# Step priorities, a decay table from one matmul, two FFN2 tiles in borrowed banks and wider warm-up matmuls in a fused attention and FFN kernel

## The chip, the cores and the metric

One core of one Trainium2 chip. Times are device microseconds of one execution of the whole kernel. Every experiment was timed beside fresh runs of the kernel before on the same chip. A ratio is the mean time of one kernel's fast runs over the mean time of the other's fast runs of the same rounds, so it is not quite the ratio of the medians quoted beside it; a bracket behind a ratio is its 95% interval. A single run counts as slow when it is more than 1.5% above the fastest run of the same kernel.

## The reference

Linear attention with a decay per head, in blocks of 64 positions, and behind it an FFN of 3072 tokens with a snake activation:

```python
# q, k, v: (4 batches, 8 heads, 768 positions, 64); lam: 8 decays near 0.98
for b in range(nb):                       # 12 blocks of 64
    intra = (qb @ kb.T * Dmask) @ vb      # Dmask[i, j] = lam ** (i - j), i >= j
    inter = (qb * lam_pow) @ kv_state
    out[block b] = intra + inter
    kv_state = lam_block * kv_state + (kb * rev_pow).T @ vb
# x: attention output as 3072 x 512; w_in 512 x 2048; w_out 2048 x 512
h = x @ w_in
g = h + sin(alpha * h) ** 2 / (alpha + 1e-9)
return g @ w_out
```

## The kernel before

The kernel cuts attention into 24 units (a batch, half of the heads, two blocks of 128 positions) and the FFN into 6 groups of 512 tokens. Four units make the input of one group. For a unit, ACT or POOL casts q and k, POOL scales v by powers of the decay (`vb`), PE turns q and k (`pt`), forms the state (`kp`, or `okv` where it uses that bank) and the scores (`sp`), DVE masks, and PE adds the inter and the intra part into `okv`. A group is 16 FFN1 tiles (`hps`), a sine, a square and a sum for each, and 4 FFN2 tiles (`ops`) of 16 matmuls each.

The Python code does not emit instructions in written order. Each step is put into a list with an estimated cost, its predecessors, the banks that it takes and a priority; a planner simulates the engines and emits each engine's steps in the order found. This matters in what follows: in the traces of this case a step that was late held up what stood behind it on its engine (ACT did no other work in the 1.36 us for which it waited for one tile, and PE none in the 1.40 us for which it waited for another, both below).

```python
class Plan:
    def run(self):
        # (cut) for each engine: of the ready steps whose banks are free,
        # take the one with the lowest priority value op.vt, and emit it
```

The decay table is made at the start from lam, which a DMA brings in. `E` holds powers of lam by position (partition) and head. The kernel needs them along the free axis on all partitions, `et`, and PE does that with 16 small fp32 matmuls, which the trace counts as x32 (two records for each of them; the prediction calls them 32 matmuls):

```python
    def tables(op):
        G.tensor_tensor(out=E[:, 0], in0=lam_bc[:], in1=pos[:].to_broadcast([P, H]), op=ALU.pow)
    def tables_v(op):
        V.tensor_tensor(out=E[:, 1], in0=E[:, 0], in1=lam_bc[:], op=ALU.mult)
        V.reciprocal(out=R[:], in_=E[:])
    def tables_t(op, hp):                 # four times, hp = 0..3
        # (cut)
        for par in range(2):
            for hd in range(2):
                h = 2 * hp + hd
                nc.tensor.matmul(out=tb0.tile[half[hd], hp, par, :],
                                 lhsT=E[:D, par, h:h + 1].to_broadcast([D, D]),
                                 rhs=idf[:], start=True, stop=True)
    def tables_l(op):                     # LBD: the decay of a whole block, needed for every state
        for hd in range(2):
            V.tensor_copy(out=LBD[half[hd], :, hd], in_=tb0.tile[half[hd], :, 1, D - 1])
```

The other parts that the change touches:

```python
    KVF = {0, 1, 2}                       # units whose state matmul uses FFN banks, not okv
    NWARM = 22; NFILL = 30; FLAG = .12    # matmuls on zeros: at the start, and in later idle time
    bd = kvp.tile([P, 2, 2, D], BF16, name=f"kvbd{b}{hh}{c}")          # decayed state
    def f2mm(op, first, g, m, j, cols=slice(0, DM)):                   # FFN2
        if j == 0:
            op.tile = bank(op, "f", [P, DM], FP32, "ops")              # one of four FFN banks
        # (cut)
```

## Time and profile before

| | kernel before |
|---|---|
| time | 220.83 us median of 3 runs (220.65 to 220.99) |
| span in the profile | 218.9 us |
| first FFN1 matmul | 22.5 us |
| start of the part in which PE has no gap | 76.4 us |
| last matmul ends | 214.8 us |

The prediction below shows how the page, the chain, the stretches and the waits of PE were read. One part of the start-up got less attention in it than it deserved, so here it is. In the timeline of a kernel each line has the start, the length, the engine, the source line, the operation, output and input names, shapes and the number of instructions; a bracket tells how long the engine sat idle just before, and whose end released it. First PE, then DVE:

```profile
6.67 1.15 PE L323 MATMUL et<-idf,E 64*64 64x64 f32 x32
7.75 0.40 PE L399 MATMUL pt<-iden,qk 128*128 128x128 bf16 x4
8.26 0.32 PE L456 MATMUL kp<-vb,qk 64*64 64x64 bf16 x16
```

```profile
7.86 0.33 DVE L329 COPY LBD<-et 64x4 f32<-64x4 f32 x2 [0.93 <-PE et L323]
```

The table is on its way at 6.67 us and `LBD` is there from 7.86. The first unit's state matmul (`kp`) follows at 8.26. PE does not idle in these lines.

### The profile page before, as it was taken

What the parts mean: (1) busy time and instruction counts of PE and PEld (TensorE: products, weight loads), DVE (VectorE), ACT (ScalarE), POOL (GpSimd) and SP (SyncE); (2) the same over time, 40 slices, a digit from 0 to 9 for tenths busy, and PEclk for the clock granted to TensorE, in tenths of its full rate; (3) what the DMA queues carried; (4) which work ended last, traced back from release to release, by engine and by line L of the source; (5) the groups of instructions that cost most, each with busy time, mean ns of one, the idle gap of its engine ahead of it and who ended that gap; (6) DMA issues with size and microseconds to landing.
All of it is one profiled execution on the core that took longest, in us unless ns stands there. A gap on an engine that the chain in (4) does not pass through costs nothing.

```text
span 218.9 us, 5315 instructions
## 1 busy us (share of the span) xinstructions
PE 207.5 (95%) x2083; PEld 108.4 (50%) x2109; DVE 121.2 (55%) x191; ACT 144.4 (66%) x255; POOL 123.1 (56%) x202
## 2 busy tenths in 40 slices
PE   8888998999999899999999999999999999999992
PEld 5656543455454354545545545554554444444461
DVE  1575986446475793777547647547646544354000
ACT  3867798873688747777567677686767676786120
POOL 5659999849869999999997545303111101101000
PEclk9999999999999999999999999999999999999998
DMA  4999999999999996893999953532022022210423
GB/s 126 293 283 251 206 199 207 261 278 268 211 202 259 218 267 129 240 279 77 197 273 230 267 144 76 47 72 48 5 48 49 1 49 48 48 32 19 96 64 81
DMA packets 62809, 33.65 MB, mean 154 GB/s; under 512 B 18608, under 2 KB 59840, under 8 KB 62784
## 3 DMA queue, kind: packets, MB, share of 16 engines
q1 hardware_dynamic: 57776, 29.04, 59.0%
q0 software_dynamic: 4752, 4.19, 12.0%
q8 instruction: 16, 0.26, 0.5%
q10 hardware_dynamic: 256, 0.08, 0.2%
q14 instruction: 9, 0.07, 0.1%
HBM read 27.28 MB, written 6.29 MB: 153 GB/s over the span
## 4 chain that ended last, share of the span: by engine, by line
PE 80%; POOL 6%; DMA 6%; issue 2%; ACT 2%; DVE 2%; SPq 1%; ACTq 0%; POOLq 0%
PE ops L603 38%; PE hps L575 33%; DMA st_v<-in_v_dram 3%; PE sp L422 3%; DMA st_q<-in_q_dram 3%; PE okv L545 2%; PE okv L532 2%; POOL vb L386 2%; POOL s L591 1%; PE okv L456 1%; PE pt L399 1%; DVE gall L594 1%; POOL kvbd L484 1%; SPq L364 1%; PE bz L654 1%
## 5 line engine op out<-in xcount | busy, mean ns | idle before, releaser
L594 DVE SCALAR_TENSOR_TENSOR gall<-s,r_sb,hps 128x512 bf16<-128x512 bf16 x96 | 70.6, 746 | 62.5 <-ACT s L589 43.8
L575 PE MATMUL hps<-xt,w_in_sb 128*128 128x512 bf16 x364 | 93.5, 379 | 2.2 <-DVE gall L594 1.0
L603 PE MATMUL ops<-w_out_sb,gall 128*128 128x512 bf16 (+1 forms) x394 | 93.6, 370 | 0.5 <-PE okv L456 0.2
L582 ACT ACTIVATE s<-hps,alpha_sb 128x512 bf16<-128x512 f32 x96 | 65.2, 684 | 34.6 <-PE hps L575 32.9
L603 PEld LDWEIGHTS <-gall 128*128 128x128 bf16 x400 | 38.6, 98 | 42.5 <-issue 0.3
L575 PEld LDWEIGHTS <-w_in_sb 128*128 128x128 bf16 x384 | 35.9, 98 | 43.3 <-issue 2.3
L591 POOL TENSOR_TENSOR s<-s 128x512 bf16<-128x512 bf16 x23 | 23.8, 1039 | 43.9 <-ACT s L582 43.8
L589 ACT ACTIVATE s<-s 128x512 bf16<-128x512 bf16 x73 | 45.7, 630 | 2.0
L431 DVE TENSOR_TENSOR sm<-sp,mask 128x512 bf16<-128x512 f32 x48 | 32.4, 684 | 3.9 <-PE sp L422 3.6
L386 POOL TENSOR_TENSOR vb<-st_v,R 128x512 bf16<-128x512 f32 x24 | 25.0, 1045 | 3.9 <-DMA st_v<-in_v_dram 3.7
L484 POOL TENSOR_TENSOR kvbd<-kvx,LBD 128x256 bf16<-128x256 f32 x32 | 19.6, 612 | 4.3 <-PE okv L532 1.8
L481 POOL TENSOR_TENSOR kvx<-kva,kvs 128x128 f32<-128x128 f32 x32 | 14.5, 454 | 13.1 <-ACT kva L466 12.9
L609 ACT COPY ob<-ops 128x512 f32<-128x512 f32 x23 | 13.2, 573 | 10.2 <-PE ops L603 6.6
L562 DVE TENSOR_TENSOR xt<-okv,ET 128x512 bf16<-128x512 f32 x24 | 16.4, 685 | 4.1 <-PE okv L545 3.6
L380 POOL CAST qk<-st_k 128x512 bf16<-128x512 f32 x20 | 12.2, 610 | 3.5 <-DMA st_k<-in_k_dram 3.5
L380 POOL CAST qk<-st_q 128x512 bf16<-128x512 f32 x16 | 9.8, 610 | 4.8 <-PE okv L456 4.4
L654 PE MATMUL bz<-zeros 128*128 128x256 bf16 x52 | 11.1, 336 | 1.1 <-DVE warm L274 1.1
L466 ACT COPY kva<-okv 128x256 f32<-128x256 f32 (+1 forms) x16 | 5.1, 318 | 9.7 <-PE okv L456 9.7
L405 ACT COPY qt<-pt 128x512 bf16<-128x512 bf16 x14 | 8.1, 587 | 4.2 <-PE pt L399 4.0
L532 PE MATMUL okv<-qt,kvbd 128*128 128x128 bf16 x80 | 8.8, 219 | 1.5 <-POOL kvbd L484 1.0
L545 PE MATMUL okv<-sm,vb 64*64 64x128 bf16 x384 | 9.9, 218 | 0.2 <-issue 0.2
L422 PE MATMUL sp<-qt 64*64 64x128 bf16 x384 | 10.0, 222 | 0.0
(50 smaller groups left out, 96.7 us busy)
## 6 DMA issues: line engine op xcount, KB each, us to landing
st_q<-in_q_dram SPq DMA_DIRECT2D x24, 256.0 KB, 5.3
st_k<-in_k_dram SPq DMA_DIRECT2D x24, 256.0 KB, 5.5
st_v<-in_v_dram SPq DMA_DIRECT2D x24, 256.0 KB, 5.2
out_dram<-ob SPq DMA_DIRECT2D x46, 128.0 KB, 2.4
w_out_sb<-in_moe_w_out_dram POOLq DMA_DIRECT2D x4, 512.0 KB, 15.6
w_in_sb<-in_moe_w_in_dram POOLq DMA_DIRECT2D x3, 512.0 KB, 10.0
w_in_sb<-in_moe_w_in_dram POOLq DMA_DIRECT2D x1, 384.0 KB, 6.5
qt<-qk SPq DMA_TRANSPOSE x15, 4.4
```

Source lines behind the costliest of these rows:

```text
L380: ENGINE[op.eng].tensor_copy(out=o, in_=i)
L386: ENGINE[op.eng].tensor_tensor(out=T[u, "vb"][:], in0=T[u, "v"][:].rearrange("p h two e -> p two h e"), in1=R[:, :, hs].unsqueeze(3).to_br ...
L422: nc.tensor.matmul(out=T[u, "sp"][hd][half[c], par, hp, :], lhsT=QT[half[hd], 1, par, hp, half[c]], rhs=QT[half[hd], 0, :, hp, half[c]], s ...
L431: V.tensor_tensor(out=T[u, "sm"][:, hd], in0=T[u, "sp"][hd][:], in1=mask[:].unsqueeze(2).to_broadcast([P, 2, 2, P]), op=ALU.mult)
L484: G.tensor_tensor(out=bd[:], in0=X.unsqueeze(2).to_broadcast([P, 2, 2, D]), in1=LBD[:, hs, :].unsqueeze(3).to_broadcast([P, 2, 2, D]), op= ...
L562: V.tensor_tensor(out=xt[g][:, 2 * hh:2 * hh + 2, bb, :, :].rearrange("p hp c i -> p c hp i"), in0=T[u, "op"][:, :, 0:2 * P].rearrange("p ...
L575: op.ins = nc.tensor.matmul(out=op.tile[:, cols], lhsT=w_in_sb[:, c, f * P:(f + 1) * P], rhs=xt[g][:, c].rearrange("p b c i -> p (b c i)") ...
L582: A.activation(out=op.tile[:, cols], in_=mm.tile[:, cols], func=ACTF.Sin, scale=alpha_sb[:, f:f + 1])
L589: A.activation(out=op.tile[:, cols], in_=s1, func=ACTF.Square)
L591: ENGINE[op.eng].tensor_tensor(out=op.tile[:, cols], in0=s1, in1=s1, op=ALU.mult)
L594: V.scalar_tensor_tensor(out=gall[g][:, f, cols], in0=sq.tile[:, cols], scalar=r_sb[:, f:f + 1], in1=mm.tile[:, cols], op0=ALU.mult, op1=A ...
L603: op.ins = nc.tensor.matmul(out=first.tile[:, cols], lhsT=gall[g][:, f, m * P:(m + 1) * P], rhs=w_out_sb[:, f, cols], start=(f == 0), stop ...
```

## The change

The intent is a shorter way from the start to the point where PE is filled with FFN work alone: better step order by a searched table of priority offsets (`TUNE`, some 700 entries; the second value of an entry, where there is one, ties the step to one engine), a table with fewer PE instructions, fewer users of the one attention output bank pair `okv`, and two FFN2 tiles of group 0 in that pair, so that FFN1 keeps its four banks. Cut to its core:

```diff
+    TUNE = {
+        "tab1": (-33.2, None), "tab2": (9.5, None), "tabd": (8.9, None), ...   # cut: some 700
+    }
+    TT = -38; TD = -500                      # priorities of the new table steps
-    NWARM = 22; NFILL = 30; FLAG = .12
+    NWARM = 11; NFILL = 20; FLAG = .25       # the 11 have 512 columns instead of 256
-    KVF = {0, 1, 2}
+    KVF = {0, 1, 2, 3, 4, 5}
-    GATES = {8: ('f', 2), 6: ('o', 0)}       # loads of unit 6 wait for w_out's first quarter
+    GATES = {8: ('f', 8), 5: ('o', 4)}       # loads of unit 5 wait for its second quarter
+    LEND = {0: ('okv', 0), 1: ('okv', 1)}
 ...
-    def tables_t(op, hp):                    # the 16 matmuls shown above
+    def tables_d(op):
+        for hd in range(2):
+            V.tensor_copy(out=E2[half[hd]], in_=E[half[hd]]
+                          .rearrange("p par (hp two) -> p two hp par", two=2)[:, hd])
+        V.tensor_tensor(out=ED[:], in0=idf[:].unsqueeze(1).to_broadcast([P, HP * 2, D]),
+                        in1=E2[:].rearrange("p hp par -> p (hp par)").unsqueeze(2)
+                        .to_broadcast([P, HP * 2, D]), op=ALU.mult)
+    def tables_t(op):
+        op.tile = bank(op, "f", [P, HP, 2, D], FP32, "et")
+        nc.tensor.matmul(out=op.tile[:].rearrange("p hp par i -> p (hp par i)"), lhsT=ones[:],
+                         rhs=ED[:].rearrange("p k i -> p (k i)"), start=True, stop=True)
 ...
-        bd = kvp.tile([P, 2, 2, D], BF16, name=f"kvbd{b}{hh}{c}")
+        bd = kvp.tile([P, 2, 2, D], BF16, name=f"kvbd{b}{hh}{c}{tp if c else 0}")
 ...
     def f2mm(op, first, g, m, j, cols=slice(0, DM)):
-        if j == 0:
+        if j == 0 and op.lent is None:
             op.tile = bank(op, "f", [P, DM], FP32, "ops")
+        elif j == 0:                         # cut: takes half of an okv pair
 ...
+    tbd = add("tabd", on("DVE", .85), [tb2], TD, tables_d)
+    tb0 = add("tab0", on("PE", .88), [tbd], TT, tables_t, take=("f",), lag=PEL, mode="n", ...)
 ...
-                for e, a in (("ACT", 2 * q), ("DVE", 3 * q)):        # last eviction in two copies
+                ev = add("end1", on("DVE", .35), [prev], vt + 4, ...) # in one
 ...
+    for op in plan.ops:
+        if op.name in TUNE:
+            by, on_ = TUNE[op.name]
+            op.vt += by
+            op.cost = [x for x in op.cost if on_ in (None, x[0])]
     for op in plan.run():
         op.emit(op)
```

Left out are the split of an early unit's output into "inter" and "out", the decay of units 0 to 2 on POOL instead of DVE, k casts on ACT, and other numbers of the planner.

## The prediction

> **What bounds the kernel now.** I read the page first: PE is busy for 95% of the span, and the chain of work that ended last is 80% PE. A busy PE is not a PE at its peak, so the second view was the timeline of PE, where the spacing of groups shows the real pace.
>
> ```profile
> span 218.9 us, 5315 instructions
> PE 207.5 (95%) x2083; PEld 108.4 (50%) x2109; DVE 121.2 (55%) x191; ACT 144.4 (66%) x255; POOL 123.1 (56%) x202
> PE 80%; POOL 6%; DMA 6%; issue 2%; ACT 2%; DVE 2%; SPq 1%; ACTq 0%; POOLq 0%
> ...
> 177.55 0.86 PE ops L603 x4
> 178.41 0.86 PE hps L575 x4
> ```
>
> The last two lines are from the chain in order of time: groups of four FFN matmuls start every 0.865 us, 216 ns each. The kernel has 6 groups x 16 tiles x 4 of FFN1 and as many of FFN2, 768 in all: 768 x 0.216 = 165.9 us. No part of the change touches that. From 76.4 us to the last matmul at 214.8 us the PE timeline has no gap: only FFN groups and attention steps of 1.01 us. So all that can be won lies before 76.4 us or behind 214.8 us.
>
> Third view, busy time by stretches (the second answer is the warm-up tile `bz` alone):
>
> ```profile
> 6.20:22.50 16.30, 14.22 (x336) 10.09 (x335) 11.31 (x24) 11.92 (x27) 11.86 (x15) 1.00 1.19 272
> 22.50:36.40 13.90, 12.79 (x131) 6.07 (x123) 10.87 (x18) 11.93 (x23) 12.93 (x20) 1.00 1.24 205
> 55.80:76.40 20.60, 19.05 (x225) 9.51 (x228) 13.77 (x22) 16.54 (x29) 17.89 (x30) 1.00 1.19 218
> ...
> 6.20:22.50 16.30, 5.73 (x27) 1.00 1.19 272
> ```
>
> The columns are PE, PEld, DVE, ACT, POOL, clock, DMA share and GB/s. From 6.2 us (first transposes) to 22.5 us (first FFN1) PE looks 87% busy, but 5.73 us of that is warm-up on zeros. In 22.5 to 36.4 us ACT (86%) and POOL (93%) are close to full too: they could become the next bound.
>
> Fourth, the timeline of PE shows the waits that PE really has:
>
> ```profile
> 17.61 0.32 PE L456 MATMUL okv<-vb,qk 64*64 64x64 bf16 x16 [0.50 <-POOL vb L386]
> 18.92 0.27 PE L532 MATMUL okv<-qt,kvbd 128*128 128x128 bf16 x2 [0.22 <-ACT kva L510]
> 20.69 0.27 PE L532 MATMUL okv<-qt,kvbd 128*128 128x128 bf16 x2
> ...
> 36.38 1.02 PE L575 MATMUL hps<-xt,w_in_sb 128*128 128x512 bf16 x4 [0.81 <-DVE gall L594]
> 67.68 0.34 PE L532 MATMUL okv<-qt,kvbd 128*128 128x128 bf16 x3 [0.47 <-POOL kvbd L484]
> 73.35 0.34 PE L532 MATMUL okv<-qt,kvbd 128*128 128x128 bf16 x3 [0.56 <-POOL kvbd L484]
> ```
>
> The first three lines are the way to the first FFN1: unit 3's state matmul takes the one `okv` buffer at 17.61, so the output of unit 2, whose second mask was done at 16.8, starts only at 18.92; its eviction ends at 20.3, and unit 3's output follows at 20.69. One buffer passes three users in turn.
>
> [...]the first 24 warm-ups of 256 columns took 5.08 us, 212 ns each, later ones near 110 ns[...] Here unit 3's v took 6.64 us to land, against a median of 5.2 us of its kind, with the first weight load issued 1.0 us after it.
>
> **The change, part by part.**
> 1. *State matmuls of units 3 to 5 in FFN banks (units 0 to 2 have them there already), early output split into "inter" and "out".* Unit 3 no longer holds `okv`. I work the way anew: v3 lands at 16.4 as before; the scaling by R 1.05 gives 17.56; state matmul 0.35 to 17.95; decay on DVE 0.43 to 18.45; inter and out 0.6 behind the masks (unit 3's transposed k is there at 17.3, scores 0.4, two masks 1.3: 19.05) to 19.5; eviction 0.69 to 20.2. The first full FFN1 tile starts at 20.3 instead of 22.5: 2.2 us. The first weight load moves behind unit 2's scaling, so v3 may land up to 1 us earlier; I count none of it. But work done before 22.5 now (unit 4's transposes, scores and state) partly slides behind. By waste: before, 16.3 us less 6.4 (four units at about 1.6), 1.3 (units 4 and 5) and 1.15 (table) is 7.4 us wasted; after, 20.3 - 6.2 = 14.1 less 6.4, 0.9 table, 0.8 of unit 4 and 0.4 for the half FFN1 tile is 5.6. **Gain 1.8**, from 1 to 3.
> 2. *Loads reordered.* Unit 5 waits for the second quarter of w_out, where before unit 6 waited for the first. One unit less is 0.79 MB, 2.7 us at the 290 GB/s of the first stretches, by which the weights come earlier. FFN1 of tile 1 now waits for its weights till about 24; this lets the 1.8 us stand. No own gain.
> 3. *Two FFN2 tiles of group 0 in the two `okv` banks.* FFN1 keeps all four FFN banks while these two tiles accumulate; FFN2 matmuls fill the waits for `gall`. It can remove the 0.81 us at 36.38. **Gain 0.7.** Price: no attention step can use `okv` until both are evicted.
> 4. *Decay tiles of chunk 1 with their own buffer per step.* POOL idled 1.82 us before a decay at 62.99 because PE still read the old one; the next two PE waits, 0.47 and 0.56, are for such tiles. **Gain 0.9.**
> 5. *Priorities, some 700 offsets.* They move no work on or off the kernel, only order. PE idles 2.6 us between 22.5 and 76.4, 1.6 of it counted above. By difference PE spends 2.5 us more there on changes between kinds of work: 138.4 us after 76.4 less 12.8 of steps is 581 FFN matmuls, so 187 x 0.216 = 40.4 us lie in the 53.9, with 8.2 of attention and 0.2 of warm-up. An order fitted to this may take 1.5 of the 3.5 left. **Gain 1.0** after a deduction for an order that fits the planner better than the chip.
> 6. *Table by one matmul.* It removes 32 matmuls (1.15 us) and adds a DVE product of about 0.7 us and one fp32 matmul of 512 columns, 0.9 us by the change's own step cost; no row of the trace has it. The table stands some 0.8 us later, at 9.7 us, and unit 0's eviction needs it at 12.0. **No change.**
> 7. *Tail.* The last two evictions run one after the other (0.27 on ACT, 0.29 on DVE, from 214.79 to 215.38). One DVE copy of 256 columns, about 0.35: **gain 0.2.** The flight of the last output, 3.5 us, stays.
>
> Sum 1.8 + 0.7 + 0.9 + 1.0 + 0.2 = 4.6. I add 0.3 for an earlier v3: 220.8 - 4.9 = **215.9 us**.
>
> **Rivals.** *A. ACT takes PE's place.* All k casts of units 1 to 7 go to ACT, 0.62 us each, where before POOL did some, and the first three states are copied there. ACT already has 86% in the stretch where FFN1 starts; an FFN1 tile wants 0.69 for the sine and 0.63 for the square, 1.32 against PE's 0.865 unless POOL squares. Against it: FFN2 can fill PE once w_out is there, and in 43 to 55 us ACT idles for want of FFN1. If it holds, parts 1 and 5 are lost: about 218.5. *B. The lent banks block attention.* Units 5 to 7 come late now, and `okv` is away: group 1 could start later than today's 55.8. For it: there is one `okv` only. Against it: PE has enough to do, 27.6 us of group 0's FFN, until unit 7 is there, and unit 5 to 7's loads need only 7 to 9 us. It would give 217.5. *C. The loads stay the bound.* DMA runs at 270 to 296 GB/s from 5 to 20 us, and no order of PE makes v3 land earlier. Then only the turn through `okv` is gained: 217. *D. The search hit well*: nearly all idle time and a third of the start-up waste go, 213.5.
>
> **Range and chances.** The parts sum to 215.9, the rivals lie at 217 to 218.5 and at 213.5; eight in ten: 213.6 to 218.6. The 2% line is 220.83 x 0.98 = 216.4, only 0.5 above my centre, so 0.57 faster, 0.41 same. Slower by 2% would need 4.4 us of new waits in a kernel that has under 3 of PE idle time after 22.5: 0.02.
>
> **What would show it.** Right: the first full FFN1 tile at 19.5 to 21 us in the PE timeline; unit 2's output before 18; no PE wait for `gall` above 0.5 near 36; no PE wait for `kvbd` at 60 to 76; the point from which PE has no gap well before 76. Wrong: an ACT or `gall` wait in 20 to 40 us, a PE gap where `okv` is lent, v3 landing later than 16.4, or warm-up matmuls running again behind the first FFN1; and, for the other side, an end below 213.

## The result, and the profile after

The changed kernel took **219.44 us** (median of four runs, 218.51 to 219.60) against 220.74 us of the kernel before (220.59 to 220.99). The ratio is 0.9931 [0.9902, 0.9961]: 0.7% faster, where 2.2% had been predicted; that is short of the 2% line and outside the range on record. A repetition with more runs said nearly the same (below).

The page and the stretches of the changed kernel (columns as in the prediction; the last line is `bz` alone):

```profile
span 217.5 us, 5238 instructions
...
PE 82%; DMA 8%; POOL 4%; ACT 2%; DVE 2%; issue 0%; DVEq 0%; ACTq 0%; POOLq 0%
```

```profile
6.20:22.50 16.30, 13.47 (x302) 8.57 (x303) 12.89 (x28) 10.53 (x27) 12.88 (x17) 1.00 1.13 242
22.50:36.40 13.90, 12.51 (x74) 5.50 (x72) 9.45 (x15) 11.87 (x21) 12.96 (x24) 1.00 1.21 205
55.80:76.40 20.60, 20.05 (x280) 10.48 (x279) 15.96 (x24) 15.71 (x29) 19.73 (x31) 1.00 1.10 241
...
6.20:22.50 16.30, 4.56 (x19) 1.00 1.13 242
```

The last stretch is what was hoped for: PE 97% busy, before 92%. But in 22.5 to 36.4 us, where FFN1 should stand closer, PE is *less* busy (12.51 us, before 12.79; a second profile of the changed kernel has 13.25 there). The PE timeline of the changed kernel shows why:

```profile
9.58 1.10 PE L601 MATMUL et<-ED,ones 128*128 128x512 f32 x2 [1.40 <-DVE ED L595]
10.61 0.32 PE L736 MATMUL kp<-vb,qk 64*64 64x64 bf16 x16
...
21.62 1.93 PE L855 MATMUL hps<-xt,w_in_sb 128*128 128x256 bf16 x12
24.67 4.49 PE L855 MATMUL hps<-xt,w_in_sb 128*128 128x512 bf16 x20 [0.66 <-DMA w_in_sb<-in_moe_w_in_dram]
29.60 3.61 PE L855 MATMUL hps<-xt,w_in_sb 128*128 128x512 bf16 x16 [0.44 <-DVE gall L874]
33.50 1.04 PE L891 MATMUL okv<-w_out_sb,gall 128*128 128x512 bf16 x4 [0.29 <-DMA w_out_sb<-in_moe_w_out_dram]
46.54 0.40 PE L676 MATMUL pt<-iden,qk 128*128 128x128 bf16 x4 [0.72 <-ACT qk L655]
62.63 1.02 PE L855 MATMUL hps<-xt,w_in_sb 128*128 128x512 bf16 x4 [0.55 <-DVE gall L874]
```

Each line but the second and the third begins with a wait that the kernel before did not have. The first is the earliest of them and the longest: PE stands 1.40 us for `ED`, the DVE product of the new table, and the first unit's state matmul comes at 10.61 instead of 8.26. FFN1 begins at 21.62 us instead of 22.5, with one tile in halves, so the first tile that is not in halves comes at about 22.5, the same as before. (The twelve matmuls of that line are eight of the halves and four of the next tile: 8 x 0.108 us, half of the 216 ns of 512 columns, puts the next tile at 22.5, an estimate.) In the profile of the repetition the waits for `ED` (1.39 us), `gall` (0.44 and 0.55) and the q cast (0.72) are there too, the one for w_in is not, and FFN1 begins at 21.27. DVE, then POOL, in the same place:

```profile
7.87 1.56 DVE L595 TENSOR_TENSOR ED<-idf,E 128x512 f32<-128x512 f32 x1
10.72 0.33 DVE L606 COPY LBD<-et 64x4 f32<-64x4 f32 x2 [0.95 <-PE et L601]
```

```profile
7.84 1.04 POOL L663 TENSOR_TENSOR vb<-st_v,R 128x512 bf16<-128x512 f32 x1 [0.33 <-DVE E L593]
```

The product took 1.56 us, not "about 0.7 us". It starts 0.03 us behind POOL's scaling of v, which runs for 1.04 us. `LBD` is there at 10.72, 2.9 us later than before. Only about half of that is the table itself, as an experiment shows: in this run of the changed kernel lam also landed later (the power on POOL began at 5.16 us, before at 4.45). That differs from run to run: the repetition of the change had 4.82.

To compare stretches I counted PE's useful work. Its records overlap (in the first lines shown above that of `et` ends at 7.82 us and the next starts at 7.75), so I took the weight loads of every kind in a stretch, times the steady spacing of that kind, without those of zeros; what is left of the stretch is time without useful work. The differences between kernels are good to about 0.4 us; the levels depend on the spacings taken, and a recount put some of them over 1 us higher. `old_table` is the experiment that follows.

| stretch, us | before | after | `old_table` |
|---|---|---|---|
| 6.2 to 22.5 | 9.3 | 8.4 | 7.65 |
| 22.5 to 36.4 | 1.2 | 1.8 | 0.6 |
| 36.4 to 55.8 | 0.1 | 0.55 | 1.2 |
| 55.8 to 76.4 | 1.3 | 0.1 | 0.0 |
| sum | 11.9 | 10.85 | 9.45 |

So 0.9 us are won ahead of 22.5 us and 0.6 of them given back by 36.4; 0.45 more are given back by 55.8; only the last stretch has its gain. The sum, 1.05 us, and the tail, 0.17 us (one copy of 0.42 us from the last matmul on where two took 0.59), make 1.2; the medians differ by 1.3. For `old_table` the same sum gives 2.6 of 3.3 us.

### The profile page after: what moved, and what is told of

It is laid out like the page before. It is cut to its first block, busy times and chain, and to the rows that moved or that the text cites. A ratio compares the mean times of both kernels' runs of the same rounds, so it can differ in the third digit from the quotient of the medians.

```text
span 217.5 us, 5238 instructions
## 1 busy us (share of the span) xinstructions
PE 206.0 (95%) x2062; PEld 104.5 (48%) x2062; DVE 123.2 (57%) x199; ACT 142.8 (66%) x256; POOL 122.3 (56%) x202
## 4 chain that ended last, share of the span: by engine, by line
PE 82%; DMA 8%; POOL 4%; ACT 2%; DVE 2%; issue 0%; DVEq 0%; ACTq 0%; POOLq 0%
PE ops L891 35%; PE hps L855 34%; DMA w_out_sb<-in_moe_w_out_dram 6%; PE okv L891 3%; PE sp L702 3%; PE okv L825 2%; DMA lam_bc<-in_lam_dram 2%; PE okv L812 2%; POOL w_in_sb L624 1%; POOL vb L663 1%; PE pt L676 1%; PE okv L736 1%; POOL E L584 1%; DVE ED L595 1%; POOL kvbd L764 1%; PE et L601 1%
## 5 line engine op out<-in xcount | busy, mean ns | idle before, releaser
L874 DVE SCALAR_TENSOR_TENSOR gall<-s,r_sb,hps 128x512 bf16<-128x512 bf16 (+1 forms) x97 | 70.0, 740 | 59.1 <-ACT s L869 46.9
L855 PE MATMUL hps<-xt,w_in_sb 128*128 128x512 bf16 (+1 forms) x388 | 90.4, 377 | 1.7 <-DVE gall L874 1.0
L891 PE MATMUL ops<-w_out_sb,gall 128*128 128x512 bf16 (+1 forms) x368 | 82.8, 370 | 0.0
L862 ACT ACTIVATE s<-hps,alpha_sb 128x512 bf16<-128x512 f32 (+1 forms) x97 | 64.5, 677 | 26.9 <-PE hps L855 25.6
L871 POOL TENSOR_TENSOR s<-s 128x512 bf16<-128x512 bf16 (+1 forms) x23 | 23.5, 1022 | 45.1 <-ACT s L862 44.8
L869 ACT ACTIVATE s<-s 128x512 bf16<-128x512 bf16 (+1 forms) x74 | 45.8, 626 | 1.7
L657 POOL CAST qk<-st_k 128x512 bf16<-128x512 f32 x17 | 10.4, 611 | 0.0
L682 ACT COPY qt<-pt 128x512 bf16<-128x512 bf16 x11 | 6.4, 587 | 5.7 <-PE pt L676 5.6
L939 PE MATMUL bz<-zeros 128*128 128x256 bf16 (+1 forms) x31 | 8.8, 371 | 1.3 <-DVE warm L541 1.2
L802 POOL TENSOR_TENSOR kvs<-kvx,ET 128x128 f32<-128x128 f32 x24 | 9.4, 402 | 0.0
```

Of the source, the lines that this page charges most:

```text
L657: ENGINE[op.eng].tensor_copy(out=o, in_=i)
L855: op.ins = nc.tensor.matmul(out=op.tile[:, cols], lhsT=w_in_sb[:, c, f * P:(f + 1) * P], rhs=xt[g][:, c].rearrange("p b c i -> p (b c i)") ...
L862: A.activation(out=op.tile[:, cols], in_=mm.tile[:, cols], func=ACTF.Sin, scale=alpha_sb[:, f:f + 1])
L869: A.activation(out=op.tile[:, cols], in_=s1, func=ACTF.Square)
L871: ENGINE[op.eng].tensor_tensor(out=op.tile[:, cols], in0=s1, in1=s1, op=ALU.mult)
L874: V.scalar_tensor_tensor(out=gall[g][:, f, cols], in0=sq.tile[:, cols], scalar=r_sb[:, f:f + 1], in1=mm.tile[:, cols], op0=ALU.mult, op1=A ...
```

## The experiments

My theory after the two traces was that step 6 of the prediction had failed: the product is slow beside POOL, PE's queue waits for it, and the whole start-up slides. The rivals were that the offsets or the lent banks cost what the rest gains, or that the new waits near 46 us and behind it carry the loss.

**The changed kernel again, five rounds.** No edit.

> The changed kernel once more, unedited, as the yardstick of the runs beside it: 0.993 of the kernel before, 219.2 to 219.6 us, with a span of 217.5 to 217.8 us. If it came out over 1 us away from that, differences under 1 us between kernels would not be readable here.

Measured: 219.28 us median of 11 runs (217.33 to 220.99, one of them slow), ratio 0.9912 [0.9879, 0.9946]. The result stands. New is the spread: 3.7 us, or 3.3 without the slow run, where 45 runs of the kernel before lay within 1.8.

**The old table in the changed kernel.** The planner keeps its costs, so that the order of all steps stays as it was; only what two steps emit differs. The product is still made, once, early and of ones, and nothing reads it: its own time can be seen that way.

```diff
+    V.memset(E2[:], 1.0)
+    V.tensor_tensor(out=ED[:], ...)          # the same product, at the start, unused
     def tables_d(op):
-        # copies into E2, product into ED
+        pass
     def tables_t(op):
         op.tile = bank(op, "f", [P, HP, 2, D], FP32, "et")
-        nc.tensor.matmul(out=..., lhsT=ones[:], rhs=ED[:]..., start=True, stop=True)
+        # the 16 matmuls of before
```

> The changed kernel with every engine's order kept, but the eviction table made by the 32 small matmuls of before; the wide DVE product stays as a measurement, moved on constants to about 3 us, where DVE and GpSimd both have nothing to do. Theory T (the table's lateness, 2.9 us at the decay table, is what ate the gain at the start): LBD is written near 8.8 us instead of 10.7, unit 0's state matmul comes near 8.5 instead of 10.6, the time falls by 0.6 to 1.5 us. Rival P (GpSimd's queue and the landing of the second w_in part near 24.6 us set the first FFN1 tiles): the first microseconds improve, FFN1 still waits to about 24, the time falls by under 0.4 us. The product by itself: 0.6 to 0.7 us if the 1.56 us in the changed kernel came from GpSimd working beside it, 1.5 us if it is the operation itself.

Measured: 217.49 us (four runs from 217.44 to 217.62, one slow one of 221.10), ratio 0.9845 [0.9817, 0.9872]. Its DVE timeline, then its PE timeline:

```profile
2.99 0.69 DVE L592 TENSOR_TENSOR ED<-idf,E 128x512 f32<-128x512 f32 x1 [0.86 <-POOL idf L563]
...
9.38 0.33 DVE L609 COPY LBD<-et 64x4 f32<-64x4 f32 x2 [1.05 <-PE et L603]
```

```profile
20.62 1.91 PE L858 MATMUL hps<-xt,w_in_sb 128*128 128x256 bf16 x11
22.92 4.49 PE L858 MATMUL hps<-xt,w_in_sb 128*128 128x512 bf16 x20
```

The same product takes 0.69 us here, with POOL idle from 2.96 to 5.19 us. `LBD` comes 1.34 us earlier than in the changed kernel (the other 1.5 us of its delay stay: they are the later lam and the new order), the first FFN1 tile 1.00 us earlier, and the DMA wait of 0.66 us is gone from the line at 22.92 (as it is in the repetition of the change). lam was as late here as in the changed kernel (5.19 us), so the gain at the start is the table's. By the medians of the fast runs the kernel is 1.7 us faster than the repetition of the change, in the same rounds.

**The reverse: the new table in the kernel before.**

```diff
-    # 16 matmuls into et
+    # E2 and ED on DVE right behind the reciprocal, one matmul with ones
```

> The kernel before with the table by one matmul and nothing else. The product now starts before GpSimd's scaling of unit 0 and not after it[...]. Theory T: the table stands 1.0 to 1.4 us later and the time rises by 0.4 to 1.2 us. Rival (the start of the kernel before is set by the loads of unit 3, so a late table is absorbed): within 0.2 us of the kernel before.

Measured: 221.93 us (22 runs), ratio 1.0040 [1.0022, 1.0057], that is 0.9 us slower. Part of this is a low clock that came more often (a mean below 0.995 in 8 of the 22 runs, in 5 of 43 of the kernel before); the means of the other runs, 221.43 and 220.89, differ by 0.5. DVE, then POOL:

```profile
6.99 0.69 DVE L327 TENSOR_TENSOR ED<-idf,E 128x512 f32<-128x512 f32 x1
```

```profile
7.27 1.31 POOL L397 TENSOR_TENSOR vb<-st_v,R 128x512 bf16<-128x512 f32 x1 [1.01 <-DMA st_v<-in_v_dram]
```

Here DVE began first, and now the product is quick and POOL's scaling is long: 1.31 us instead of 1.04. Adding up: 6.99 + 0.69 = 7.68, and 7.68 + 1.04 = 8.72, close to the 8.58 at which it ended. In the changed kernel POOL began first: 7.84 + 1.04 = 8.88, and 8.88 + 0.69 = 9.57, close to 9.43. In both, the second ends within 0.14 us of where it would end if it began only when the first was done (an estimate from the lengths of 0.69 and 1.04 us). The new table costs time even in this order. Its `LBD` came at 8.96 us instead of 7.86, but how that reaches the end is not shown: in this one trace FFN1 began at 21.86 us, earlier than the 22.51 of the kernel before.

A later run (`one_decay_buffer`, below) has the order of the changed kernel at the start, and yet its trace shows the other outcome. DVE, then POOL:

```profile
7.46 0.69 DVE L595 TENSOR_TENSOR ED<-idf,E 128x512 f32<-128x512 f32 x1
```

```profile
7.46 1.58 POOL L663 TENSOR_TENSOR vb<-st_v,R 128x512 bf16<-128x512 f32 x1 [0.37 <-DVE E L593]
```

By the record DVE was 0.01 us ahead here, and the product was the quick one; in the other four profiles with this order at the start (two of the change and the two without offsets) POOL was 0.03 to 0.04 us ahead, and the product took 1.55 to 1.56 us. PE then waited 0.39 us for `ED` instead of 1.40. So in these five profiles the product was quick where it started first and slow where POOL started 0.03 to 0.04 us ahead of it. Whether this is a part of its spread was not tested.

**The new table, product first.** If the order decides, then the change can keep its table when DVE makes the product ahead of the reciprocal for which POOL waits.

```diff
     def tables_v(op):
         V.tensor_tensor(out=E[:, 1], in0=E[:, 0], in1=lam_bc[:], op=ALU.mult)
-        V.reciprocal(out=R[:], in_=E[:])
+        # E2 copies and the product into ED, from tables_d
+        V.reciprocal(out=R[:], in_=E[:])
```

> The changed kernel with its table by one matmul and every order kept except on DVE: the product stands ahead of the reciprocal that GpSimd's scaling of unit 0 waits for, so GpSimd cannot be reading then. [...] the table matmul starts near 8.3 us instead of 9.6, the scaling of unit 0 0.6 to 0.9 later, and the time falls by 0.4 to 1.2 us against the changed kernel. If it stays within 0.3 of the changed kernel, the product's collision is not what costs.

Measured: 217.77 us (217.31 to 220.33), ratio 0.9882 [0.9839, 0.9925]. DVE, POOL and PE:

```profile
7.47 0.69 DVE L592 TENSOR_TENSOR ED<-idf,E 128x512 f32<-128x512 f32 x1
```

```profile
8.41 1.04 POOL L664 TENSOR_TENSOR vb<-st_v,R 128x512 bf16<-128x512 f32 x1 [1.37 <-DVE alpha_sb L618]
```

```profile
8.73 1.13 PE L602 MATMUL et<-ED,ones 128*128 128x512 f32 x2
```

Both instructions have their own length now, and `et` starts 0.85 us earlier than in the changed kernel, though POOL's scaling starts 0.57 later. About half of the 0.85 is chance: lam landed 0.43 us earlier in this run (power on POOL at 4.73 us). The median is 1.4 us better than that of the change's fast runs. Two of the six runs are above 219.8 us, with a mean clock of 0.989, so the interval of the ratio still touches that of the change. Among runs with a mean clock of 0.995 or more the means are 217.6 us here (4 of 6), 217.5 with the old table (4 of 5) and 218.7 for the repetition of the change (6 of 11): by these few runs the order of the product gets back what the old table does.

**The offsets off.** The change without `TUNE`.

```diff
-        if op.name in TUNE:
+        if False:
```

> The changed kernel with the per-step priorities taken out (the scheduler falls back on its hand-made ones) and all else kept. If the offsets give what I forecast for them (1.0 us) or more, it runs at 220.4 us or above. If the order that they make costs time on the chip, it runs below 219.

Measured: 220.18 us (22 runs, one slow), ratio 0.9964 [0.9946, 0.9981]. The offsets are worth 0.5% or about 1.1 us (0.9964 against 0.9912, of some 220). The step that gave them 1.0 us had about the right size, though the two intervals meet at 0.9946 and the time is just under the 220.4 us set in advance; they do not cost the gain.

**No own decay buffer for each step.**

```diff
-        bd = kvp.tile(..., name=f"kvbd{b}{hh}{c}{tp if c else 0}")
+        bd = kvp.tile(..., name=f"kvbd{b}{hh}{c}0")
```

> The changed kernel with every engine's order kept, but the decay tiles of chunk 1 with one buffer for all steps, as before. If step 4 of the prediction is right, GpSimd waits again for PE ahead of its decays between 60 and 76 us, PE waits for decay tiles near 67 and 73 us, and the time rises by 0.5 to 1.2 us. Rival (the new order alone removed those waits, the buffer does nothing): within 0.3 us of the changed kernel.

Measured: 218.83 us (19 runs, one slow), ratio 0.9895 [0.9871, 0.9918], not distinct from the change. Its trace has no PE or POOL wait for `kvbd` between 55 and 77 us either. So those waits are gone, as predicted, but not by the buffer. Nor are they back in the trace without offsets. Which part of the change removed them stays open.

**Nothing lent.** With the offsets on, the plan without `LEND` was found to deadlock before it could run, so here nothing is lent and the offsets are off as well; it is to be compared with the run without offsets.

```diff
-    LEND = {0: ('okv', 0), 1: ('okv', 1)}
+    LEND = {}
```

> The changed kernel without per-step priorities and without the two lent FFN2 tiles, to be held against the one without priorities alone (220.2 us), because without lending and with the priorities the order runs into a deadlock. If lending is worth what I forecast (0.7 us), it runs at 220.7 to 221.2; if lending costs (FFN2 is used up before group 1 starts, and PE waits for gall there), it runs at 219.9 or below.

Measured: 220.83 us (22 runs), ratio of the fast runs 0.9954 [0.9930, 0.9978], against 0.9964 with lending: in fast runs no effect on the time can be told. But seven of these 22 runs are slow (221.98 to 224.85 us), against one of the 22 with lending; over all runs the means are 221.1 and 220.2 us. Whether lending spares the kernel slow runs, or the rounds differed, was not tested. The waits of PE between 22.5 and 80 us (engine, tile, what it waited for: us in total, times, longest), nothing lent and then lent, both without offsets:

```profile
PE hps L855 <- DVE gall L874: 2.5, 7, 0.7
```

```profile
PE hps L855 <- DVE gall L874: 0.8, 2, 0.5
```

With lending there are 1.7 us less of waits for `gall`, but new waits of PE beside them (0.7 us for a q cast, 0.6 for `okv`), and all of PE's waits in that stretch sum to 2.7 us in both. That fits fast runs that take the same time.

**The q cast ahead of the lent tiles' evictions.** After `old_table` the largest wait was 0.72 us of PE for a q cast. PE and then ACT of `old_table`:

```profile
44.71 0.40 PE L679 MATMUL pt<-iden,qk 128*128 128x128 bf16 x4 [0.72 <-ACT qk L658]
```

```profile
43.55 0.59 ACT L900 COPY ob<-okv 128x512 f32<-128x512 f32 x1 [1.36 <-PE okv L894]
44.03 0.62 ACT L658 CAST qk<-st_q 128x512 bf16<-128x512 f32 x1
```

ACT sat idle 1.36 us for a lent tile, evicted it, and only then made unit 6's cast. Two experiments on top of `old_table`: one puts the casts of unit 6 ahead of both evictions in ACT's queue; the other lets unit 5 load earlier, in case the data were late.

```diff
+    move(order, "ev_0_1", "cq6")             # old_table_swap: emitted behind the casts of unit 6
+    move(order, "ev_0_0", "ck6")
```

```diff
-    load(op, u, 0, gate)                     # unit 5, gate: w_out's second quarter
+    load(op, u, 0, gate_of(("o", 0)))        # old_table_gate0: its first quarter
```

> The kernel with the 32 small table matmuls, and on ACT alone two evictions of the lent FFN2 tiles moved behind the casts of unit 6's q and k that stand after them. There PE waited 0.72 us near 44.7 us for the q cast, which stood in ACT's queue behind an eviction that itself waited 1.36 us for PE. Theory Q (the lent tiles hold ACT's queue): that PE wait goes and the time falls by 0.4 to 0.8 us against the old-table kernel, to about 216.9. Rival L (unit 6's q lands only then): the wait stays, the time is the same within 0.2.

> The kernel with the 32 small table matmuls and every order kept, but unit 5's loads wait for the first quarter of w_out instead of the second. Theory L (attention of units 5 to 7 comes late because of their loads): the loads start some 2.5 us earlier, PE's wait near 44.7 shrinks, FFN1 of group 1 starts before 56.6, and the time falls by 0.3 to 1 us. Rival D ([...]w_out lands later by as much): FFN2 waits for w_out near 32 us, the time is the same or up to 1 us worse.

Measured: with the casts first the wait is gone from the trace (of a slow run; the fast profile of `combined`, which has the same two moves, doesn't have it either), and three fast runs took 216.40, 217.98 and 218.52 us, ratio 0.9845 [0.9801, 0.9889], the same as `old_table`; the other three were slow ones at 219.93 to 221.28. With the early loads 218.35 us, ratio 0.9881 [0.9845, 0.9917], and the wait stayed at 0.7 us. So the queue of ACT makes the wait, not the data, as theory Q said, but without the 0.4 to 0.8 us that it promised: what removing the wait gives the time is hidden in the spread.

**Combined.** The old table, the casts first, and unit 4's state matmul behind the two halves of the first FFN1 tile, because in slow profiles PE waited there (below).

```diff
+    move(order, "kv4", "f1_0_0_1")           # with its decay and its copy behind it
```

> The 32 small table matmuls, the two evictions behind unit 6's casts, and on PE unit 4's state matmul behind the two half FFN1 tiles instead of ahead of them. In the profiled run of the swap PE stood 1.98 us ahead of the first FFN1 tile for unit 4's v, which that run brought late. If that is what spreads the times of the changed kernels from run to run, the spread shrinks and the median falls to 216.4 to 217.2; PE's wait near 44 us for the q cast is gone and the first half tile of FFN1 starts at 20.3 or before. If the spread has another cause, the fastest runs are near 216.5 and the spread stays.

Measured: 219.11 us (217.95 to 219.66), ratio 0.9917 [0.9894, 0.9940], a miss. The spread shrank to 1.7 us, but a new wait came at 23 us in the PE timeline, because a copied state is now made later:

```profile
23.13 1.02 PE L858 MATMUL hps<-xt,w_in_sb 128*128 128x512 bf16 x3 [0.82 <-ACT kva L793]
```

**The old table again, for a look at a slow run.**

> The kernel with the 32 small table matmuls once more, as the yardstick of this call: 217.5 us in most runs, with single runs up to 221 as the first time.

Measured: 217.54 and 218.00 us, and two slow ones of 221.09 and 221.19, ratio of the fast ones 0.9851 [0.9822, 0.9881]. The profiled run was a slow one. POOL, PE, and stretches of 3 us of it:

```profile
21.65 1.04 POOL L666 TENSOR_TENSOR vb<-st_v,R 128x512 bf16<-128x512 f32 x1 [2.52 <-DMA st_v<-in_v_dram]
```

```profile
22.74 0.43 PE L739 MATMUL kp<-vb,qk 64*64 64x64 bf16 x16 [2.16 <-POOL vb L666]
```

```profile
20.00:23.00 3.00, 0.84 (x40) 0.62 (x42) 1.05 (x2) 0.11 (x1) 1.35 (x2) 0.89 1.24 204
23.00:26.00 3.00, 2.92 (x39) 1.93 (x31) 1.71 (x3) 1.55 (x5) 2.66 (x4) 0.54 1.19 211
```

Unit 4's v was scaled at 21.65 us, in the fast profile at 19.05. PE's queue waits 2.16 us for it, and behind that the granted clock is 0.54 for three microseconds. In the slow profile of `old_table_swap` the wait is 1.98 us, and the granted clock is 0.86 and 0.80 in the two stretches of 5 us from 20 us on. The wait and some 1.4 us from the lower clock (an estimate: 3 us at 0.54) account for the 3.6 us between the two groups of runs. What brings the clock down these traces alone do not show. The ratios use fast runs alone.

**Work on zeros in that place.** To see whether the idle PE brings the clock down:

```diff
     def kvmm_first(op, u):
+        if u == 4:
+            bz = bank(op, "f", [P, DM], FP32, "bz")
+            for _ in range(12):
+                nc.tensor.matmul(out=bz[:, :2 * P], lhsT=zeros[:, :P], rhs=zeros[:, :2 * P], ...)
```

> The kernel with the former decay table again, and ahead of the state matmul of unit 4 twelve matmuls of 256 columns on zeros, in the same order otherwise: work for TensorE while it waits for unit 4's v. Twelve at 0.11 us are 1.3 us. Theory W: runs of the slow group are those in which that v lands 2 us late, TensorE stands 2.2 us, and the clock falls behind it. Then the runs with v in time lose up to 1.3 us (217.5 becomes 218.3 to 218.8), the slow group comes down to at most 219.8, and no run has a mean clock under 0.995. Rival X: the clock falls for some other reason (a late landing costs what it costs, and the fills do nothing for the clock): the slow group stays at 221 or goes to 222, with mean clocks of 0.984 to 0.992 as before.

Measured: 218.97 us (218.67 to 219.99, six runs), ratio 0.9924 [0.9897, 0.9951]. No run is slow and no mean clock is below 0.995. Of the 21 runs of the four `old_table` kernels without these matmuls (`old_table`, its repetition, the swap and the earlier loads) seven were slow, with mean clocks of 0.988 to 0.992, so six runs without a slow one would come by chance about one time in eleven, (14/21) to the sixth. That speaks for the theory and does not prove it, and the profiled run was one in which v was in time. The price is seen in the PE timeline:

```profile
20.43 1.48 PE L729 MATMUL bz<-zeros 128*128 128x256 bf16 x12
```

The fill costs the fast runs 1.5 us, so it is a probe and no improvement. (One run of the kernel before in these rounds took 540.88 us and is left out.) The best version by fast runs stays `old_table`, 217.5 us, 1.5% faster than the kernel before and faster than the change. But three of its nine runs were slow. With these counted in, its mean is 218.8 us, that of the eleven runs of the change 219.3: half a microsecond is left.

## Why the prediction was wrong

**Step 6 failed.** It reads: "The table stands some 0.8 us later, at 9.7 us, and unit 0's eviction needs it at 12.0. **No change.**" Two things in it were wrong. The size: "a DVE product of about 0.7 us" measured 1.56 beside POOL's scaling (0.69 in the one profile in which DVE was just ahead). (The fp32 matmul of 512 columns, put at 0.9 us, leaves two records that span 1.10, 1.13 and 1.10 us in three kernels, the change, `product_first` and `before_new_table`, and the next matmul starts 1.03, 1.06 and 0.93 us behind the first of the two. The 16 matmuls of 64 columns that it replaced took 1.15 us.) And the consumer: I compared the table with the last step that needs it, the eviction, while in PE's fixed queue the table matmul stands ahead of the first state matmul and the first scores, which don't need it. PE stood 1.40 us, the first unit's state matmul came 2.3 us later than before, and the units after it followed. Taking the table away from the change gives 1.5 us by the ratios (0.9912 and 0.9845, a difference of 0.0067 of 220.8 us), 1.7 us by the medians of fast runs, and 1.1 us among runs with a mean clock of 0.995 or more; adding it to the kernel before costs 0.9 us, 0.5 at such a clock. This is the largest single term of the miss, and without it the kernel lies at 217.5, inside the range.

**Step 1, the shorter way to FFN1, fits the traces, but no run changed it alone.** It had unit 3's eviction start at 19.5 us. With the old table it starts at 20.09, in the change at 21.15, in the kernel before at 21.39 (one profile each). With the old table the first two stretches lose 8.25 us to idle PE or zeros, against 10.5 before: 2.25 us, predicted 1.8. In the change itself only 0.3 us of it is left, because the table holds the start up and, in this profile, the second part of w_in lands late (0.66 us at 24.67). Rival C named the loads as the bound; that fits this one wait, which the repetition did not have.

**Step 2** said "No own gain"; the loads were not separated from the rest by any run, so the 0.3 us added for an earlier v3 stays an estimate. Unit 5's earlier release changed nothing for the better.

**Step 3, lending, 0.7 us.** The traces without offsets show 1.7 us less of waiting for `gall`; the times of fast runs show nothing. Rival B was partly right: FFN1 of group 1 starts at 58.45 us, later than the 55.8 of before, FFN2 of group 0 is used up at 57.9, and a wait of 0.55 us for `gall` follows at 62.63.

**Step 4, decay buffers, 0.9 us.** The size fits (55.8 to 76.4 us: 1.2 us less without useful work, and PE has no gap from 63.6 us on), the cause does not: the waits stay away without the buffers, and what removed them is open.

**Step 5, priorities, 1.0 us.** Measured about 1.1, with wide intervals. The entries do not change the order alone, as the step says: some also tie a step to an engine.

**Step 7, the tail, 0.2 us.** Measured 0.17.

**The rest.** The sum of the gains was 4.9 us, measured 1.3 to 1.9; the table is 1.1 to 1.7 of the gap. The others are the new waits, which the prediction allowed for only as rivals: 0.72 us for the q cast behind a lent tile's eviction (rival A's engine, but by its queue and not by its load: ACT was 68% busy between 36.4 and 55.8), 0.44 and 0.55 for `gall`, 0.29 for w_out. They add up to 2.0 us of PE idle time, against the one wait of 0.81 us near 36 us that went. That is about the size of the remainder; only the q cast was tested, and what each is worth in time stays open. So is what the wider warm-up did by itself: no run changed it alone. (The 11 wide ones took 3.79 us in the profile of the change and 4.69 in that of `old_table`; in the kernel before, the first 24 of 256 columns took 5.08.)

Of the signs set in advance, the first full FFN1 tile failed (22.5 us, not 19.5 to 21), and a `gall` wait at 29.60 and a PE gap at 46.54, both called signs of being wrong, came; unit 2's output before 18 us (17.79) and the absence of the `gall` wait near 36 and of the `kvbd` waits came as well.

## What to carry to other kernels

Before a PE job is replaced by a DVE job plus a shorter PE job, look in the trace at what POOL does in that very microsecond: here the DVE product took 0.69 us when it started ahead of POOL's scaling and 1.56 us when it started 0.03 us behind it. Where PE waits for such a DVE instruction, let it start first, and by more than the 0.01 to 0.04 us that lay between the two here, in either order. A late step costs what stands behind it in its engine's queue, not only what depends on it (PE stood 1.40 us for the product, with a state matmul behind it that does not need the table), so the slack of a step is to be read from the queue. And a schedule that is tighter around DMA landings can have a better median and a wider spread (3.7 us over the 11 runs of the change's repetition, 1.8 over 45 of the kernel before): look at all the runs and their clocks, not at the median of the fast ones alone.
